# Fewer and reordered DMA transfers in a two-layer attention and SwiGLU kernel

## The chip, the core and the metric

The kernel runs on one core of a Trainium2 chip. The metric is the device time of one execution in microseconds (us); three runs of the kernel before were timed, and one execution was profiled. The core has five engines with an instruction queue each: PE (TensorE, with its weight loads shown as PEld), DVE (VectorE), ACT (ScalarE), POOL (GpSimd) and SP (SyncE, which here only issues DMA transfers). Transfers issued from SP, ACT and POOL are carried by the core's 16 DMA engines.

## The reference

Two layers of the same pair of blocks are applied to x, 2048 tokens of 1024 numbers, all in float32: softmax attention with 32 heads of 32, then a routed SwiGLU block that changes only the eight tokens with the highest router score.

```python
def _A_ref(x, wqkv, wo):
    B, S, D = x.shape
    H = 32; Dh = D // H
    qkv = (lambda x, *d: x.transpose(*d))((x @ wqkv).reshape(B, S, 3, H, Dh), 2, 0, 3, 1, 4)
    q, k, v = qkv[0], qkv[1], qkv[2]
    scale = Dh ** -0.5
    scores = jnp.einsum("bhqd,bhkd->bhqk", q, k) * scale
    p = _softmax(scores, axis=-1)
    o = jnp.einsum("bhqk,bhkd->bhqd", p, v)
    return (lambda x, *d: x.transpose(*d))(o, 0, 2, 1, 3).reshape(B, S, D) @ wo

def _B_ref(x, w_r, w_gate, w_up, w_down):
    C = 8
    r = x @ w_r
    idx = jnp.argsort(-r, axis=-1)[:, :C]
    ...
    g = _silu(x_sel @ w_gate)
    u = x_sel @ w_up
    y = (g * u) @ w_down
    r_sel = _sigmoid(jnp.take_along_axis(r, idx, axis=1))
    ...
    return x + upd.reshape(B, S, D)

x = A_x
x = x + _A_ref(_layernorm(x, axis=-1), A_wqkv, A_wo)
x = x + _B_ref(_layernorm(x, axis=-1), B_w_r, B_w_gate, B_w_up, B_w_down)
x = x + _A_ref(_layernorm(x, axis=-1), A_wqkv, A_wo)
x = x + _B_ref(_layernorm(x, axis=-1), B_w_r, B_w_gate, B_w_up, B_w_down)
```

## The kernel before

The order of the work is written out by hand: what a Python loop emits first stands first in its engine's queue. Each layer goes through three stages.

**Projections** (`steps`, 96 of them, step k, or chunk c and place b = k % 24). For each of four chunks of 512 tokens the weight matrix wqkv passes in 12 blocks of 1 MB, two steps to a block. `load_w` (L105 is its DMA, tile `wraw`) fetches a block two blocks ahead, at the even steps; ACT rounds it to a high part (L827 or L831) and POOL takes the low part (L832), and PE multiplies both with the normalised tokens (L932). Queries, keys and their low parts go back to DRAM (qh, ql, kh, kl) and come in again as `q` and `ks` for attention. Beside the projections of layer 1 the SwiGLU block of layer 0 runs (`prev`): its weights come as 1 MB tiles `fw` in five buffers (L237), in groups of four. `tick` and `refill` load a new tile for each one used; after a group of four uses at k % 4 == 3, three loads are issued there and the fourth by the `refill` of the next step.

**Attention.** 32 units, each four heads by 512 queries, against 16 blocks of 128 keys: scores (L775), exponentials on ACT (L1256), values (L1154), and row maxima ahead of time (L736). The softmax sums of a unit are formed by `sum_mm` (L1201) as one row per head, on partitions 0, 32, 64 and 96 of tile `sm`, and `store_sum` writes them to DRAM tensor `sd`. Near the end the sums are loaded in a dense form, turned into reciprocals and stored as `rd`, for each tile of 128 tokens [4, 8, 128]: four heads by eight groups by 128 tokens.

**Output projection.** 16 tiles of 128 tokens (t). `load_o(t)` brings the attention output `oT` (512 KB) and the reciprocal sums into tile `ord` (two buffers); a row of rd, 4 KB, is repeated over the 32 partitions of its head. Loads 0 to 3 are issued from SP; in the loop ACT issues the load of t + 4 right after it has rounded tile t + 2. DVE scales (L1360), ACT rounds (L1369), DVE takes the low part (L1372), PE multiplies with wo (L1438, 48 matmuls a tile into one of two PSUM buffers `pre`), and DVE adds x (L1443), takes layer-norm sums (L177), normalises (L1470) and forms the router score (L1472), whose last use frees the PSUM buffer. SP loads x for t + 2 and stores the new x for t (L1480), and between t = 1 and 4 (layer 0) or 1 and 10 (layer 1) a SwiGLU tile of 1 MB.

Of the kernel before, what the change touches and what calls it, by code (L numbers as in the profile page):

```python
# [21 lines left out]
NG = H // 4  # L22
# [31 lines left out]

KEYS_AT = [{at: slice(i * 512, i * 512 + 512) for i, at in enumerate(ats)} for ats in (
    ((1, 18), (1, 21), (2, 18), (3, 3)), ((2, 14), (2, 17), (2, 20), (3, 3)))]


def unit_events(left):
# [17 lines left out]
def tile_kernel(ctx, tc, x, wqkv, wo, w_r, w_gate, w_up, w_down, out):  # L77
# [3 lines left out]
    def sbuf(name, bufs=1, side=None):  # L81
        kw = {"side": side} if side else {}
        return tc.tile_pool(name=name, bufs=bufs, reuse_waits="tile", **kw)
# [19 lines left out]
    def dma(out, in_):  # L103
        f = [a.bitcast(F32) if a.dtype == F32R else a for a in (out, in_)]
        sync.dma_start(f[0], f[1])  # L105
# [4 lines left out]
    def ps_pre():  # L110
        return psum.tile([128, 1024], F32, name="pre", bufs=2)
# [556 lines left out]
    def layer(n, src, dst, prev=None, following=None):  # L668
# [6 lines left out]
        sd = dram.tile([NT, 4, NG, 128], F32, name=f"sd{n}")  # L675
        sd2 = dram.tile([NT, 4, NG, 128], F32, name=f"se{n}")
        rd = dram.tile([NT, 4, NG, 128], F32, name=f"rd{n}")
# [8 lines left out]
        def open_qk():  # L686
            side = "right" if prev else None
            qp = mid.enter_context(sbuf(f"q{n}", side=side))
            for i in range(3):
                QP.append(qp.tile([128, 2, 2, 512], F32R, name=f"q{i}", bufs=1))  # L690
            KS[0] = right.enter_context(sbuf(f"ks{n}", side="right")).tile([128, 2, 2, S], F32R, name="ks0")
# [9 lines left out]
        q_loads = [(b, i) for i in range(3) for b in range(2)]  # L701

        def load_q(u, j):
            g, qc = divmod(u, QC)
            if j == 0:
                Q[u] = QP[u % 3]
            b, i = q_loads[j]
            r = 64 * b + 32 * (i % 2)
            dma(Q[u][r:r + 32, :, i // 2, :],
                (ql if i == 2 else qh)[g, :, qc * 512:(qc + 1) * 512].rearrange("(p b r) c -> b r p c", p=2, b=2)[b])  # L710
# [91 lines left out]
        with ExitStack() as pst:  # L802
# [5 lines left out]
            def load_w(wb):  # L808

                RAW.append((wb, pr_.tile([128, 2048], F32, name="wraw")))  # L810
                if wb < 8:
                    w = wqkv[:, wb * 256:(wb + 1) * 256]
                else:
                    v, h = divmod(wb - 8, 2)
                    w = wqkv[h * 512:(h + 1) * 512, 2 * D + v * 512:2 * D + (v + 1) * 512]
                w = w.rearrange("(a p) c -> p a c", p=128)
                dma(RAW[-1][1].rearrange("p (a c) -> p a c", a=w.shape[1]), w)

            def split_w(parts=1):
                wb, raw = RAW.pop(0)  # L820

                wh, wl = (prev.wf.tile([128, 2048], F32R, name=i) for i in ("ord", "ohl")) if n else (
                    pr_.tile([128, 2048], F32R, name=i) for i in ("wh", "wl"))
                W[wb] = [w.rearrange("p (a c) -> p a c", a=KD if wb < 8 else 4) for w in (wh, wl)]
                sls = [slice(2048 // parts * i, 2048 // parts * (i + 1)) for i in range(parts)]
                for sl in [slice(0, 2048)] if n else []:
                    act.copy(wh[:, sl], raw[:, sl])  # L827
                    yield
                for sl in sls:
                    if not n:  # L830
                        act.copy(wh[:, sl], raw[:, sl])  # L831
                    pool.tensor_tensor(wl[:, sl], raw[:, sl], wh[:, sl].bitcast(F32), op=OP.subtract)  # L832
                    yield

            def ln_load(t):
                XT[t] = pr_.tile([128, D], F32, name="xt", bufs=4)
                for part, rows in rows_of(src, t):
                    dma(XT[t][part], rows)
# [3 lines left out]
            def ln_stat(t):  # L842
                LS[t] = ln_stats(XT[t])
# [12 lines left out]
            def ln_store(t):  # L856
                act.dma_start(xd[t], XN[t])

            def ln_quarters(t):

                for q in range(4):
                    act.dma_start(XT[t][32 * q:32 * q + 32].rearrange("r (g c) -> r g c", g=4),
                                  xd[t].rearrange("(g r) (q c) -> q r g c", g=4, q=4)[q])
# [188 lines left out]
            for k, (c, wb, i) in enumerate(steps):  # L1052
                b = k % 24
                if prev:
                    if k == 1:
                        yield
                        pw = pst.enter_context(sbuf(f"pj{n}", bufs=2))
                        routing = prev.second_stage()
                    if k >= 3:
                        next(routing, None)  # L1060
                    if k == 22:
                        moves = prev.permutation()
                    if k in (22, 23):
                        next(moves)
                    if k % 4 == 0:
                        prev.refill()
                    if k == 60:
                        assert not prev.steps
                        ln_load(NT - 1)
                        prev.close()  # L1070
                        open_qk()
                j = k // 2 + 1
                if i == 0 and j < len(blocks):
                    if j > 1:
                        list(split_w())
                        if j + 1 < len(blocks):
                            load_w(blocks[j + 1][1])

                at = b - (1, 8 if n else 7)[c == 0]
                t = 4 * (c + 1) + at // 4  # L1080
                norm = c < 3 and 0 <= at < 16
                if norm and at % 4 == 0:
                    ln_stat(t)
                    (ln_norm if n else ln_norm_split)(t)
                if norm and at % 4 == 1 and not n:
                    ln_store(t)
                if norm and at % 4 == 2 and not n:
                    ln_quarters(t)
                if wb < 8:
                    proj(wb, i, c, c == 3 and b >= 6)  # L1090
                else:
                    proj_v(wb, i, c, c == 3, norm_rest if k == 0 else None)
                if prev and k % 4 == 3 and 11 <= k < 60:
                    if prev.steps and prev.steps[0][0] == "t":
                        prev.tick()
                    for j in range(4):
                        if not (j and prev.steps and prev.steps[0][0] == "y"):
                            prev.tick()
                if norm and n and at % 4 == 2:
                    ln_tr(t, True)()  # L1100
                    if t + 4 < NT - 1:
                        ln_load(t + 4)
                if norm and not n and at % 4 == 3:
                    ln_turn(t)
                    if t + 2 < NT:
                        ln_load(t + 2)
                if (c, b) in KEYS_AT[n]:
                    for j in range(3):
                        for h in range(4):
                            load_k(0, h, j, KEYS_AT[n][c, b])  # L1110
                if (c, b) == (2, 20):
                    load_ones(0)
                    for u in range(2):
                        for j in range(len(q_loads)):
                            load_q(u, j)
            assert not pairs
        if prev:
            prev.wf_end.close()
# [3 lines left out]
        with sbuf(f"at{n}", bufs=2) as aw:  # L1122
# [87 lines left out]
            def store_sum(u, p, t):  # L1210
                (dve.tensor_copy if PLAIN <= u <= NU - 3 else act.copy)(t, p)
                g, qc = divmod(u, QC)
                for h in range(4):
                    dma(sd[4 * qc:4 * qc + 4, h, g, :], t[32 * h:32 * h + 1, :].rearrange("p (t c) -> p t c", t=4))

            def sum_out(u):
                store_sum(u, sum_mm(u), aw.tile([128, 512], F32, name="sm", bufs=1))
# [76 lines left out]
            for s in [*range(threes), *range(threes, NS, 3), *range(NS, NS + 14)]:  # L1294
# [27 lines left out]
                t = s - 1 if s < NS - LEAD else s - 2  # L1322
# [18 lines left out]
        if True:  # L1341
            OR, RD, OT, X = {}, {}, {}, {}

            def load_o(t, eng=act):
                tile = wf.tile([128, 2048], F32, name="ord").rearrange("p (k a c) -> p k a c", k=2, a=NG)
                OR[t], RD[t] = tile[:, 0], tile[:, 1]
                eng.dma_start(OR[t], oT[t])
                for h in range(4):
                    eng.dma_start(RD[t][32 * h:32 * h + 32], rd[t, h:h + 1].to_broadcast([32, NG, 128]))

            def halves_o():
                tile = wf.tile([128, 2048], F32R, name="ohl").rearrange("p (k a c) -> p k a c", k=2, a=NG)
# [70 lines left out]
            for t in range(NT - 2 if n else NT):  # L1423
                oh, ol = OT.pop(t)
                p = ps_pre()
# [61 lines left out]
        if n:  # L1487
# [3 lines left out]
            p = [[waste[:, h] for h in halves], [ps_st(), ps_pv()]]  # L1491
# [72 lines left out]
            for i in range(2):  # L1564
                t = NT - 2 + i
# [40 lines left out]
```

## Time and profile before

| | us |
|---|---|
| three runs | 4342.66, 4354.69, 4354.86 |
| median | 4354.69 |
| the profiled execution | 4348.58 |
| its span in the profile | 4346.8 |
| PE busy in the span | 4307.6 |
| POOL, DVE, ACT busy | 3270.6, 3045.8, 2880.2 |

The profile shows one execution. A row of a group gives line, engine, operation, out<-in and count, then times; "x<-y" with a q after the engine (SPq, ACTq) is a DMA that this engine's queue issued, and its length is that of the issue alone. In the rows of stretches come the stretch, its length, the busy time of PE, PEld, DVE, ACT and POOL with the number of instructions in brackets, the granted TensorE clock as a share of full speed, the mean busy share of the 16 DMA engines, and the GB/s that they moved. The chain of waits follows the work that ended last back from the last instruction; its rows give start, length and what it was.

### The profile page before, as it was taken

How to read it: one execution, taken by the hardware profiler on the slowest of the kernel's cores; microseconds unless marked ns; L12 is line 12 of the kernel's file. 1: busy time of each engine (PE TensorE's matmuls, PEld its weight loads, DVE VectorE, ACT ScalarE, POOL GpSimd, SP SyncE). 2: the span in 40 equal slices, each digit the busy share in tenths (PEclk: the TensorE clock that was granted, in tenths of full speed). 3: DMA queues.
4: the chain of work that ended last, by engine and by line, in shares of the span. 5: the costliest groups of instructions: out<-in, count | busy, mean ns of one | idle time of the engine just before them, and what ended most of it. 6: DMA issues, size and time to landing. Idle time of an engine off the chain costs nothing.

```text
span 4346.8 us, 75763 instructions
## 1 busy us (share of the span) xinstructions
PE 4307.6 (99%) x28255; PEld 2612.5 (60%) x28255; DVE 3045.8 (70%) x5607; ACT 2880.2 (66%) x3447; POOL 3270.6 (75%) x1367
## 2 busy tenths in 40 slices
PE   9999999999999999999999999999999999999998
PEld 7888755555555555558877787555555555555583
DVE  3322678888888898887422215888888888888863
ACT  3333289999999999960222222999999998999510
POOL 5544479999999999925634443899999999999152
PEclk9999999999999999999999999999999999999999
DMA  7877588998999989868698774999989999998698
GB/s 222 268 241 230 158 183 190 200 204 193 210 199 192 214 191 199 174 181 244 180 313 305 263 215 129 206 196 196 210 190 201 200 195 201 198 195 175 185 266 342
DMA packets 362638, 918.70 MB, mean 211 GB/s; under 512 B 48220, under 2 KB 184924, under 8 KB 305934
## 3 DMA queue, kind: packets, MB, share of 16 engines
q0 software_dynamic: 53312, 384.39, 44.2%
q1 hardware_dynamic: 291646, 490.07, 37.2%
q10 hardware_dynamic: 17312, 39.40, 3.3%
q8 instruction: 222, 3.64, 0.3%
q14 instruction: 146, 1.20, 0.1%
HBM read 395.35 MB, written 134.67 MB: 122 GB/s over the span
## 4 chain that ended last, share of the span: by engine, by line
PE 93%; DMA 3%; DVE 1%; issue 1%; POOL 1%; ACT 0%; SPq 0%; POOLq 0%; ACTq 0%; DVEq 0%
PE pv L1154 23%; PE pre L775 22%; PE st L932 17%; PE st L736 15%; PE pre L1438 6%; PE pre L932 5%; PE st L1201 1%; PE pv L567 1%; DMA wraw<-in_A_wqkv_dram 1%; PE pre L757 1%; PE pv L932 1%; DMA ord<-rd 0%; PE third L775 0%; DMA P<-P 0%; PE st L607 0%
## 5 line engine op out<-in xcount | busy, mean ns | idle before, releaser
L1164 POOL TENSOR_TENSOR acc<-acc,P 128x2048 f32<-128x2048 f32 x420 | 2058.7, 4902 | 9.4
L1256 ACT ACTIVATE P<-pre 128x1024 f32<-128x1024 f32 x2016 | 1955.1, 1024 | 24.8 <-PE pre L775 17.6
L743 DVE TENSOR_REDUCE nm<-st 128x1 f32<-128x512 f32 x1920 | 1321.0, 688 | 51.3 <-PE st L736 7.9
L775 PE MATMUL pre<-q,ks 64*128 64x512 f32 (+1 forms) x8064 | 1123.1, 395 | 2.4 <-ACT P L1256 2.4
L1154 PE MATMUL pv<-P,v 128*32 128x512 f32 x8192 | 1087.2, 605 | 0.0
L736 PE MATMUL st<-ks,q 64*128 64x512 f32 x2880 | 874.3, 432 | 2.0 <-issue 2.0
L775 PEld LDWEIGHTS pre<-q,ks 64*128 64x128 f32 (+1 forms) x8064 | 770.5, 186 | 159.9 <-ACT P L1256 32.1
L741 DVE CUSTOM_DVE_ANT_0 first<-st,first 128x512 f32<-128x512 f32 x960 | 664.0, 692 | 241.3 <-PE st L736 231.9
L739 ACT ACTIVATE first<-st 128x512 f32<-128x512 f32 x960 | 574.5, 598 | 184.4 <-PE st L736 99.6
L736 PEld LDWEIGHTS st<-dt,q 64*128 64x128 f32 x960 | 175.7, 183 | 798.2 <-DVE nm L741 727.4
L736 PEld LDWEIGHTS st<-ks,q 64*128 64x128 f32 x2880 | 487.9, 185 | 46.0 <-issue 2.3
L736 PE MATMUL st<-dt,q 64*128 64x512 f32 x960 | 476.3, 496 | 0.0
L1192 POOL DMA_DIRECT2D P<-P x366 | 373.9, 1022 | 111.3 <-PE st L736 39.6
L947 DVE TENSOR_TENSOR lo<-st,hi 128x512 fp32r<-128x512 f32 x128 | 88.4, 691 | 513.9 <-ACT hi L946 469.0
L832 POOL TENSOR_TENSOR ohl<-wraw,ord 128x2048 fp32r<-128x2048 f32 (+1 forms) x54 | 222.3, 4120 | 241.5 <-ACT ord L827 205.7
L946 ACT CAST hi<-st 128x512 fp32r<-128x512 f32 x128 | 75.2, 587 | 444.5 <-PE st L932 352.5
L832 POOL TENSOR_TENSOR wl<-wraw,wh 128x2048 fp32r<-128x2048 f32 (+1 forms) x54 | 222.5, 4123 | 170.6 <-ACT wh L831 165.2
L1154 PEld LDWEIGHTS pv<-P,v 128*32 128x32 f32 x8192 | 164.0, 108 | 263.7 <-issue 257.0
L1164 POOL TENSOR_TENSOR acc<-P 128x2048 f32<-128x2048 f32 x62 | 317.9, 5128 | 0.1
L181 POOL TENSOR_TENSOR rs<-mv,eps_c 128x1 f32<-128x1 f32 x64 | 27.7, 433 | 296.3 <-DVE mv L179 296.3
L1438 PE MATMUL pre<-woh,ohl 128*128 128x512 f32 x960 | 223.9, 390 | 3.0 <-DVE pre L1472 2.2
L1369 ACT CAST ohl<-ord 128x1024 fp32r<-128x1024 f32 x32 | 33.6, 1051 | 273.4 <-DVE ord L1360 114.3
(422 smaller groups left out, 5317.4 us busy)
## 6 DMA issues: line engine op xcount, KB each, us to landing
P<-P POOLq DMA_DIRECT2D x366, 1024.0 KB, 10.1
wraw<-in_A_wqkv_dram SPq DMA_DIRECT2D x96, 1024.0 KB
q<-qh SPq DMA_DIRECT2D x256, 128.0 KB
ks<-kh SPq DMA_DIRECT2D x112, 256.0 KB
fw<-in_B_w_down_dram SPq DMA_DIRECT2D x17, 1024.0 KB
vd<-vn SPq DMA_DIRECT2D x32, 512.0 KB
qh<-hi SPq DMA_DIRECT2D x64, 256.0 KB
ql<-lo SPq DMA_DIRECT2D x64, 256.0 KB
```

What stands on the lines that cost most here:

```text
L736: pe.matmul(p, Q[u][rows, i, 0, qt * 128:(qt + 1) * 128], keys, start=True, stop=True, tile_position=(64 * b, 0))
L739: act.activation(side, ps[jj], AF.Relu)
L741: dve.tensor_tensor_reduce(side, ps[jj], side, 1.0, -3.0e38, OP.add, OP.max, NM[u][:, 0, h, qt:qt + 1])
L743: dve.tensor_reduce(NM[u][:, 1 + k, h, qt:qt + 1], ps[1 - jj], axis=AX.X, op=OP.max)
L775: pe.matmul(p[:, b * 512:(b + 1) * 512], KS[(u // QC) % 2][rows, i, slot, kt * 128:(kt + 1) * 128], Q[u][rows, i, slot, :], start=(slot == ...
L832: pool.tensor_tensor(wl[:, sl], raw[:, sl], wh[:, sl].bitcast(F32), op=OP.subtract)
L932: pe.matmul(p, *pair(a, l, r), start=(a == 0 and k == 0), stop=(a == KD - 1 and k == 2))
L1154: pe.matmul(PV[u][32 * h:32 * h + 32, :], V[g, kt // 4][:, kt % 4, 32 * h:32 * h + 32], P[s][:, h, :], start=(kt == 0), stop=(kt == NT - 1 ...
L1164: (dve if on_dve else pool).tensor_tensor(o, a, P[u * NT + k].rearrange("p h c -> p (h c)"), op=OP.add)
L1192: pool.dma_start(P[u * NT + a], P[u * NT + b], accum_op=OP.add)
L1256: act.activation(P[s][:, 2 * i:2 * i + 2, :].rearrange("p h c -> p (h c)"), p, AF.Exp, scale=SCALE)
L1438: pe.matmul(p[:, bl], l[:, a, :], r[a][:, bl], start=(k == 0 and a == 0), stop=(k == 2 and a == KD - 1))
```

## The change

There are four edits. In `store_sum` the four stores of a unit, one per head, become one transfer whose source steps over the four partitions. In `load_o` the four loads of rd, one per head with 32 partitions each, become one transfer into 128 partitions. In the projections `prev.refill()` moves from ahead of `load_w` to behind it. And the loads of the first two units' queries, which stood together at step (2, 20) behind the row of ones, are spread over (2, 21), (3, 1) and (3, 7), with the ones at (3, 5).

```diff
+QUERIES_AT = {(2, 21): range(0, 4), (3, 1): range(4, 10), (3, 7): range(10, 12)}
...
-                    if k % 4 == 0:
-                        prev.refill()
                     if k == 60:
                         assert not prev.steps
                         ln_load(NT - 1)
...
                         list(split_w())
                         if j + 1 < len(blocks):
                             load_w(blocks[j + 1][1])
+                    if prev and k % 4 == 0:
+                        prev.refill()
...
-                if (c, b) == (2, 20):
+                for j in QUERIES_AT.get((c, b), ()):
+                    load_q(*divmod(j, len(q_loads)))
+                if (c, b) == (3, 5):
                     load_ones(0)
-                    for u in range(2):
-                        for j in range(len(q_loads)):
-                            load_q(u, j)
...
             def store_sum(u, p, t):
                 (dve.tensor_copy if PLAIN <= u <= NU - 3 else act.copy)(t, p)
                 g, qc = divmod(u, QC)
-                for h in range(4):
-                    dma(sd[4 * qc:4 * qc + 4, h, g, :], t[32 * h:32 * h + 1, :].rearrange("p (t c) -> p t c", t=4))
+                dma(sd[4 * qc:4 * qc + 4, :, g, :].rearrange("t h c -> h t c"),
+                    t.rearrange("(h r) (t c) -> h r t c", h=4, t=4)[:, 0])
...
                 eng.dma_start(OR[t], oT[t])
-                for h in range(4):
-                    eng.dma_start(RD[t][32 * h:32 * h + 32], rd[t, h:h + 1].to_broadcast([32, NG, 128]))
+                eng.dma_start(RD[t].rearrange("p a c -> p (a c)"),
+                              rd[t].rearrange("h a c -> h (a c)")[:, None, :].to_broadcast([4, 32, NG * 128]))
```

Lines of the file move by two or three with it. In the rows below the number behind a DRAM name is its buffer's, and the sizes are those of the destination.

ACT's queue in the output projection of layer 1, from the round of tile 3 on. Before:

```order
L1369 CAST ohl<-ord 128x1024 x2
L1347 DMA ord<-oT_21184 128x1024
L1349 DMA ord<-rd_21189 32x1024 x4
L1369 CAST ohl<-ord 128x1024
L1347 DMA ord<-oT_21184 128x1024
L1349 DMA ord<-rd_21189 32x1024 x4
```

And now:

```order
L1371 CAST ohl<-ord 128x1024 x2
L1349 DMA ord<-oT_21091 128x1024
L1350 DMA ord<-rd_21096 128x1x1024
L1371 CAST ohl<-ord 128x1024
L1349 DMA ord<-oT_21091 128x1024
L1350 DMA ord<-rd_21096 128x1x1024
```

Between two rounds ACT issues two transfers where it issued five.

SP's queue in the projections of layer 1, at one group of SwiGLU tiles. Before:

```order
L105 DMA kd_21183<-diff 128x256
L237 DMA fw<-in_B_w_up_dram 128x2048 x4
L105 DMA wraw<-in_A_wqkv_dram 128x8x256
L105 DMA qh_21178<-hi 128x512
L105 DMA ql_21179<-lo 128x512
```

And now:

```order
L108 DMA kd_21090<-diff 128x256
L240 DMA fw<-in_B_w_up_dram 128x2048 x3
L108 DMA wraw<-in_A_wqkv_dram 128x8x256
L240 DMA fw<-in_B_w_up_dram 128x2048
L108 DMA qh_21085<-hi 128x512
```

The fourth SwiGLU tile has moved behind the weight block; the first three have not.

SP's queue at the end of chunk 2 of layer 1, where keys and the first queries are loaded. Before:

```order
L105 DMA ks_25496<-kh_21180 32x512 x4
L105 DMA ks_25496<-ones_row 1x2x2048 x2
L105 DMA q_25490<-qh_21178 32x2x512 x4
L105 DMA q_25490<-ql_21179 32x2x512 x2
L105 DMA q_25491<-qh_21178 32x2x512 x4
L105 DMA q_25491<-ql_21179 32x2x512 x2
L105 DMA wraw<-in_A_wqkv_dram 128x8x256
L105 DMA vd_21182<-vn 128x4x256 x2
L105 DMA wraw<-in_A_wqkv_dram 128x8x256
```

And now:

```order
L108 DMA ks_25352<-kh_21087 32x512 x4
L108 DMA q_25346<-qh_21085 32x2x512 x4
L108 DMA wraw<-in_A_wqkv_dram 128x8x256
L108 DMA vd_21089<-vn 128x4x256 x2
L108 DMA wraw<-in_A_wqkv_dram 128x8x256
```

Four query loads are left ahead of the weight block; eight, and the two of ones, have moved to later steps.

## The prediction

> **What bounds the kernel now.** I read the page first, for the engine that sets the end.
>
> ```profile
> span 4346.8 us, 75763 instructions
> PE 4307.6 (99%) x28255; PEld 2612.5 (60%) x28255; DVE 3045.8 (70%) x5607; ACT 2880.2 (66%) x3447; POOL 3270.6 (75%) x1367
> ```
>
> TensorE is busy for 99% of the span: 39.2 us are left in which any edit can gain, and most of those are the start and the tail. So I looked for the places where this change could take from those 39 us, and then for places where it could make new ones. Busy time in stretches (stretch, length, busy of PE, PEld, DVE, ACT, POOL, granted clock, DMA share, GB/s) and the waits of PE alone (total, times, longest):
>
> ```profile
> 1000.00:1020.00 20.00, 20.00 (x158) 10.29 (x154) 17.84 (x37) 18.13 (x23) 19.92 (x8) 1.00 0.86 183
> 2255.00:2260.00 5.00, 3.30 (x24) 1.28 (x17) 3.19 (x6) 2.09 (x3) 4.78 (x2) 0.96 0.87 297
> 2260.00:2265.00 5.00, 5.00 (x18) 3.96 (x17) 0.00 (x0) 1.90 (x1) 2.81 (x2) 0.70 0.82 238
> 2570.00:2575.00 5.00, 3.66 (x16) 2.73 (x15) 0.69 (x1) 2.39 (x2) 4.01 (x2) 1.00 0.68 202
> ...
> PE st L932 <- POOL ohl L832: 2.7, 2, 1.4
> PE pre L1438 <- DVE pre L1472: 2.2, 2, 1.5
> ```
>
> In attention PE has no gap (20.00 of 20.00). In layer 1's projections it lost 1.70 us near 2257, and the clock then fell to 0.70 for 5 us (1.5 us more), and 1.34 us near 2571. The releaser both times is POOL's split of a weight block (L832). The chain of waits says what the split waited for, and the DMA issues on SP (start, length) say what stood ahead of that load:
>
> ```profile
> 2235.09 2.24 SPq L237 DMA_DIRECT2D fw<-in_B_w_up_dram  x4
> 2237.38 15.15 DMA wraw<-in_A_wqkv_dram
> 2254.54 4.57 POOL ohl L832
> ...
> 2550.19 1.21 SPq L105 DMA_DIRECT2D ks<-ones_row  x2
> 2551.44 1.81 SPq L105 DMA_DIRECT2D q<-qh  x4
> 2556.11 1.28 SPq L105 DMA_DIRECT2D q<-ql  x2
> 2557.64 8.27 DMA wraw<-in_A_wqkv_dram
> 2567.97 4.60 POOL ohl L832
> ```
>
> A weight block landed 15.15 us after 2237.38 because four SwiGLU loads of 1 MB went out just ahead of it, and another was issued only at 2557.64, behind ones and queries that began at 2550.19.
>
> The other place is the output projection, where the reciprocal sums are loaded:
>
> ```profile
> 4103.75 43.95 PE pre L1438 x192
> 4101.97 8.20 ACTq L1349 DMA_DIRECT2D ord<-rd  x4
> 4110.27 1.05 ACT L1369 CAST ohl<-ord 128x1024 fp32r<-128x1024 f32 x1 [9.98 <-DMA ord<-rd]
> 4111.35 1.23 DVE L1372 TENSOR_TENSOR ohl<-ord,ohl 128x1024 fp32r<-128x1024 f32 x1 [3.05 <-ACT ohl L1369]
> ```
>
> A tile is 48 matmuls, so PE sets a pace of 43.95 / 4 = 11.0 us a tile. ACT stood 8.20 us over four rd loads before its next copy, and DVE then waited 3.05 us for that copy. The two waits of PE for L1472 (2.2 us in all) are the end of this road: DVE works in order, L1472 is late, and the PSUM buffer that it reads and writes comes free late.
>
> How full are the DMA engines there?
>
> ```profile
> 4140.00:4220.00 80.00, 78.51 (x347) 64.69 (x347) 50.08 (x65) 8.18 (x8) 40.69 (x54) 1.00 1.02 282
> 1940.00:2060.00 120.00, 119.36 (x533) 97.22 (x532) 84.42 (x127) 11.57 (x11) 66.77 (x79) 1.00 0.89 246
> 1916.50:1918.00 1.50, 1.50 (x20) 0.51 (x16) 1.50 (x2) 0.83 (x2) 0.00 (x0) 1.00 1.12 205
> 4320.00:4330.00 10.00, 7.69 (x34) 1.59 (x32) 0.00 (x0) 0.00 (x0) 0.00 (x0) 1.00 1.03 410
> ord<-rd ACTq DMA_DIRECT2D x96, 128.0 KB
> ord<-oT ACTq DMA_DIRECT2D x24, 512.0 KB
> x<-x SPq DMA_DIRECT2D x31, 512.0 KB
> out_dram<-x SPq DMA_DIRECT2D x13, 512.0 KB
> fw<-in_B_w_gate_dram SPq DMA_DIRECT2D x16, 1024.0 KB
> ```
>
> In layer 1's output projection all 16 are full (share 1.02) at 282 GB/s, 17.6 KB/us each; in layer 0's they are at 0.89. With weights alone a full engine moves 410 / 16 = 25.6 KB/us; while little but rd loads run (1916.5 to 1918) it moves 205 / 16 = 12.8.
>
> **The change part by part.** *Weight block ahead of the fourth SwiGLU load.* The first three still go out before it; the fourth moves behind it. So the block starts one 1 MB transfer earlier, 1 MB / 297 GB/s = 3.5 us, which is more than the 1.70 us that PE lost. Gain 1.70 + 1.5 = 3.2 us (if the split stays late: 0). The moved load becomes 3.5 us later; five buffers stand for groups of four, so it is used a group later, four steps after it is issued. Without that cover it would cost up to 3.5 us in each of the ten groups.
>
> *Queries and ones spread.* The block of 2557.64 loses two ones and eight of twelve queries ahead of it: of the 7.45 us from 2550.19 to 2557.64 about 5 us, more than the 1.34 us lost. Gain 1.34 us (ends: 0 and 1.34). The four queries that the first maxima need go out at (2, 21), nine steps before (3, 6), where they are read; the rest, and the ones, have as much or more. They now stand ahead of weight blocks at (3, 2), (3, 6) and (3, 8), at most six of them; I count nothing there, since all twelve with the ones and twelve key loads cost 1.34 us where they stood together.
>
> *Stored sums as one transfer.*
>
> ```profile
> L105 SPq DMA_DIRECT2D sd<-sm x248: 552/1038/1362, 621.0 to 4058.8; - x124
> L105 SPq DMA_DIRECT2D q<-nmx x128: 537/585/1248, 516.2 to 4028.5; - x128
> L105 SPq DMA_DIRECT2D nmx<-nmr x256: 302/484/1472, 511.5 to 4026.4; - x128
> L1349 ACTq DMA_DIRECT2D ord<-rd x96: 308/432/1370, 1941.4 to 4227.2; - x96
> ```
>
> SP saves about 3 x 1.04 us a unit. Nothing waits for it: PE has 20.00 of 20.00 in attention. 0 us.
>
> *Reciprocal sums as one transfer.* Here the count of pieces matters. A transfer's issue takes at least 302 to 308 ns where its outermost count is 16 or 32 (nmx<-nmr, ord<-rd), and at least 537 to 552 where it is 2 or 4 (q<-nmx, sd<-sm). The queue handles a transfer with a small outermost count in another way. The old rd load had 32 rows outermost on both sides; the new one has 128 on the SBUF side and, in DRAM, four heads outermost, each repeated 32 times. I take the +240 ns as the mark of a transfer that only as many engines share as its outermost count allows, here four. Then 512 KB rest on four engines, 128 KB on each, where each of 16 had 32 KB.
>
> The Trainium skill, "DMA: Bandwidth & Descriptors", section "Rules for kernel authors", says the same: an outermost size below 16 confines the whole transfer to at most that many engines. The issue times above fit this rule; which engines carried what no row here shows. By the rule alone the merge would be a loss wherever the engines are nearly full.
>
> What one of the four then has to do per tile: 128 KB of rd at 25.6 or 12.8 KB/us is 5.1 to 10.2 us. Beside it, a sixteenth of oT, x in, x out and a SwiGLU load (2.5 MB, so 160 KB) at 25.6 or 17.6 KB/us is 6.4 to 9.3 us; without the SwiGLU load 96 KB, 3.8 to 5.6. Sum with SwiGLU load 11.5 to 19.5, without 8.9 to 15.8, against PE's 11.0. I take the middles, 15.5 and 12.4, since twelve engines get less to do, which speeds up what is shared, while the four read and write the rd rows in the form that ran at 205 GB/s. Excess 4.5 us (ends 0.5 and 8.5) and 1.4 us (0 and 4.8) a tile. Layer 1 has ten tiles with SwiGLU loads (t = 1 to 10) and five more rd loads: 10 x 4.5 + 5 x 1.4 = 52. Layer 0 has four (t = 1 to 4) and eleven: 18 + 15 = 33. The two ord buffers let a load go out two tiles ahead of need; of that I count one tile, 11 us, in each layer as slack that is used up first: 41 and 22, in all 63 us. Ends: 0 and (109 - 11) + (87 - 11) = 174 us. A gain belongs to it too: ACT no longer stands over four issues, so the 2.2 us of L1472 go, but a later rd puts DVE in the same wait. What is late next is the scaling on DVE (L1360), then L1472, then PE.
>
> **Sum.** The profiled execution took 4348.58 us (span 4346.8), 6.1 under the median of the three runs, 4354.69. 4348.6 - 3.2 - 1.3 + 63 = 4407 us.
>
> **Rivals.** *All 16 engines carry the merged load.* For it: both sides hold the same 128 rows, and 128 divides by 16. Against it: the issue times. Then only gains are left: 3.2 + 1.3 + 2.2 = 6.7, 4342 us, not slower. It decides if the issue of the new load stays near 0.31 us. The Trainium skill, same page and section, advises to join many small transfers into one, small meaning under 64 KB; the old loads were 128 KB, and no row here shows a gain of joining as such.
>
> *Four engines, but hidden.* If rd and the rest run at 25.6 KB/us, 10 x 0.5 + 4 x 0.5 = 7 us lie within the 22 us of slack, and 4348.6 - 4.5 = 4344 us follows. Against it: the stage ran at 17.6 KB/us with all 16 at work.
>
> *Slower still.* If rd keeps 12.8 KB/us in layer 1, 98 + 22 - 4.5 = +115 us, 4464.
>
> **How the numbers follow.** Four engines with a loss that PE sees: 0.70, of it 0.10 above 4464; hidden: 0.12; all 16: 0.18. About 0.3% (13 us) is what a measurement of this kernel can tell from no change. The hidden case and most of the all-16 case (4342, -0.15%) fall within it: 0.25; 0.05 is left for faster, 0.70 for slower. The likeliest case alone spans 4365 to 4465; with the rivals the range is 4340 to 4465.
>
> **What would show it.** Right: ord<-rd issues of 0.54 us or more; DVE ord L1360 waiting for DMA ord<-rd in tile after tile; PE busy well under 78.5 of 80 us in layer 1's output projection, with a DMA share below 1, since twelve engines idle; no wait of PE for POOL L832 near 2257 and 2571. Wrong: issues near 0.31 us and a share near 1 with PE full; a new wait for wraw or fw in the projections; a gap in attention.

## The result and the profile after

The changed kernel took 4405.51 us, the median of four runs (4403.65 to 4409.8); the old one took 4354.34, the median of four as well, the three shown above and one more. The ratio is 1.0133, with a 95% interval of 1.0116 to 1.0151: slower by 1.3%. The profiled execution took 4407.05 us. Its page:

```profile
span 4405.2 us, 75347 instructions
...
PE 4322.8 (98%) x28255; PEld 2619.4 (59%) x28255; DVE 3042.6 (69%) x5607; ACT 2882.2 (65%) x3447; POOL 3268.6 (74%) x1367
...
L1440 PE MATMUL pre<-woh,ohl 128*128 128x512 f32 x960 | 237.2, 406 | 39.7 <-DVE pre L1474 39.0
```

The work of DVE, ACT and POOL is what it was. PE is idle for 82.4 us instead of 39.2, and 39.7 us of that stand before one group, the matmuls of the output projection, where PE waits for the PSUM buffer that L1474 (L1472 before) frees. PE's busy time grew too: in the three stretches with gaps below the granted clock is 0.87, 0.96 and 0.94, in the two without 1.00. Stretches of the changed kernel (columns as above; the whole program has moved by 8 us in layer 0 and 26 us in layer 1's projections):

```profile
2275.00:2295.00 20.00, 20.00 (x105) 14.29 (x104) 6.53 (x12) 5.35 (x7) 8.39 (x6) 1.00 0.98 350
2590.00:2605.00 15.00, 15.00 (x68) 12.43 (x67) 1.38 (x2) 3.56 (x4) 5.57 (x3) 1.00 0.66 181
4180.00:4260.00 80.00, 65.70 (x253) 52.50 (x252) 40.12 (x52) 6.29 (x6) 32.68 (x41) 0.87 0.78 227
...
1940.00:2060.00 120.00, 109.08 (x465) 88.75 (x464) 71.85 (x94) 10.51 (x10) 55.08 (x69) 0.96 0.74 205
...
1740.00:1800.00 60.00, 55.67 (x412) 28.45 (x408) 47.81 (x97) 49.18 (x60) 53.74 (x20) 0.94 0.81 172
```

The first two are the places of the old stalls near 2257 and 2571, now full. In the next two, the output projections, PE lacks 14.3 of 80 and 10.9 of 120 us, and the DMA share fell from 1.02 and 0.89 to 0.78 and 0.74, although each tile needs the same bytes: PE waits for data while part of the DMA engines have nothing to do. The last is attention in layer 0, where PE lacks 4.3 us that it did not lack before.

Who waits for whom in layer 1's output projection, from the issue of the new load (minimum, median and maximum in ns, first and last start) through the waits of DVE between 4070 and 4300 to a piece of the chain of waits:

```profile
L1350 ACTq DMA_DIRECT2D ord<-rd x12: 531/531/532, 4125.1 to 4272.2; - x12
```

```profile
DVE ord L1362 <- DMA ord<-rd: 47.2, 10, 7.2
DVE ord L1362 <- DMA out_dram<-x: 16.1, 2, 8.6
```

```profile
4186.90 20.32 DMA ord<-rd
4207.28 13.08 DMA out_dram<-x
...
4245.46 22.55 DMA ord<-rd
4268.03 1.23 DVE ord L1362
...
4272.18 21.36 DMA ord<-rd
```

In these three places a rd load is on its way for 20 to 23 us, where PE needs a tile every 11. DVE's scaling (L1362) waits for it ten times, 47.2 us in all. Stores of x stand in the same chain, the one shown with 13 us. They would be late for the same reason if a part of each must pass the busy engines too; which engines carried a store no row shows.

Where the 58.4 us of span went is read from the first and last start of the matmuls of the loop in each layer, before and then after:

```profile
L1438 PE MATMUL pre<-woh,ohl x512: 387/389/500, 1920.5 to 2095.4; 128*128 128x512 f32 x171
L1438 PE MATMUL pre<-woh,ohl x448: 387/389/502, 4079.9 to 4232.5; 128*128 128x512 f32 x150
```

```profile
L1440 PE MATMUL pre<-woh,ohl x512: 387/389/765, 1928.5 to 2121.4; 128*128 128x512 f32 x171
L1440 PE MATMUL pre<-woh,ohl x448: 387/389/767, 4095.7 to 4281.9; 128*128 128x512 f32 x150
```

| stretch | before | after | difference |
|---|---|---|---|
| start to layer 0's output projection | 1920.5 | 1928.5 | +8.0 |
| layer 0's output projection | 174.9 | 192.9 | +18.0 |
| from there to layer 1's | 1984.5 | 1974.3 | -10.2 |
| layer 1's output projection | 152.6 | 186.2 | +33.6 |
| from there to the end of the span | 114.3 | 123.3 | +9.0 |

The last +9.0 belongs to the rd loads as well: the products of the last two tiles stand behind the loop, and their data come late. Of the kernels below, the one with the merged load alone (merged_only) has 121.7 us there, the changed one with four rd loads again (four_loads) 114.4.

### The profile page after: what moved, and what is told of

Read it like the earlier page. It is cut to its first block, busy times and chain, and to the rows that moved or that the text cites. A ratio compares the mean times of both kernels' runs of the same rounds, so it can differ in the third digit from the quotient of the medians.

```text
span 4405.2 us, 75347 instructions
## 1 busy us (share of the span) xinstructions
PE 4322.8 (98%) x28255; PEld 2619.4 (59%) x28255; DVE 3042.6 (69%) x5607; ACT 2882.2 (65%) x3447; POOL 3268.6 (74%) x1367
## 4 chain that ended last, share of the span: by engine, by line
PE 86%; DMA 8%; DVE 2%; issue 2%; POOL 1%; ACT 0%; SPq 0%; POOLq 0%; ACTq 0%; DVEq 0%
PE pv L1156 22%; PE pre L778 21%; PE st L935 17%; PE st L739 14%; PE pre L935 6%; DMA ord<-rd 3%; DMA out_dram<-x 2%; PE st L1203 1%; DMA x<-x 1%; PE pre L1440 1%; DMA P<-P 1%; PE pv L570 1%; PE pre L760 1%; DMA x<-in_A_x_dram 1%; PE pv L935 1%
## 5 line engine op out<-in xcount | busy, mean ns | idle before, releaser
L746 DVE TENSOR_REDUCE nm<-st 128x1 f32<-128x512 f32 x1920 | 1320.8, 688 | 53.8 <-PE st L739 10.9
L184 POOL TENSOR_TENSOR rs<-mv,eps_c 128x1 f32<-128x1 f32 x64 | 37.1, 580 | 360.9 <-DVE mv L182 360.9
L1440 PE MATMUL pre<-woh,ohl 128*128 128x512 f32 x960 | 237.2, 406 | 39.7 <-DVE pre L1474 39.0
L1371 ACT CAST ohl<-ord 128x1024 fp32r<-128x1024 f32 x32 | 33.6, 1051 | 334.6 <-DVE ord L1362 308.1
```

Source lines behind the costliest of these rows:

```text
L746: dve.tensor_reduce(NM[u][:, 1 + k, h, qt:qt + 1], ps[1 - jj], axis=AX.X, op=OP.max)
L1440: pe.matmul(p[:, bl], l[:, a, :], r[a][:, bl], start=(k == 0 and a == 0), stop=(k == 2 and a == KD - 1))
```

## The experiments

The theory: a transfer's outermost count sets how many DMA engines share it, always the same ones, and with a count of 4 the four of them are busy for longer than PE's 11 us a tile. Rivals: one large transfer that signals only as a whole comes too late, whoever carries it; or the other edits have a part in the loss.

**The changed kernel with four rd loads** (four_loads).

```diff
-                eng.dma_start(RD[t].rearrange("p a c -> p (a c)"),
-                              rd[t].rearrange("h a c -> h (a c)")[:, None, :].to_broadcast([4, 32, NG * 128]))
+                for h in range(4):
+                    eng.dma_start(RD[t][32 * h:32 * h + 32], rd[t, h:h + 1].to_broadcast([32, NG, 128]))
```

> The changed kernel with the four rd loads per tile of the old kernel, its other three edits kept. If the whole loss is the merged rd load (engines theory): 4.5 us of gain are left, 4350 us beside 4354.5, a ratio of 0.999, PE back to over 78 of 80 us in layer 1's output projection, no wait of PE near 2257 and 2571. If part of the loss belongs to the moved refill, the queries or the joined stores of the sums: slower than the old kernel by that part; the 4.3 us in which PE waited for q near 1770 in the changed kernel would then be there again.

4347.72 us beside 4351.56, ratio 0.9995 (0.9985 to 1.0006). The loss is gone, so it is the rd load's. The 4.5 us of gain can't be told from nothing, and PE's wait for q near 1770 stayed (4.3 us): that part does not belong to the rd load.

**The old kernel with the merged rd load alone** (merged_only): the reverse of that diff, applied to the old kernel.

> The old kernel with the one merged rd load per tile, nothing else changed. If the engines that carry the merged load are the whole cause: the loss of the changed kernel and its missing gains of 4.5 us, so +51 to +56 us, 4406 to 4410, and the waits near 2257 and 2571 are there as before. If the edits only lose together: less than +30 us.

4409.86 us, ratio 1.0141 (1.0122 to 1.0161), +58 us: the one edit brings the whole loss, somewhat more than expected. One thing came otherwise: of the two old stalls at weight blocks only the second is there (1.8 us, near 2597). The first is gone, though this kernel has neither the moved refill nor the spread queries.

**One transfer, 16 rows outermost** (copies_16). The 512 KB into 128 partitions stay one transfer; only the source is laid out differently.

```diff
-        rd = dram.tile([NT, 4, NG, 128], F32, name=f"rd{n}")
+        rd = dram.tile([NT, 4, 4, NG, 128], F32, name=f"rd{n}")
...
-                dma(half_of(rd, i), t)
+                for k in range(4):
+                    dma(rd[i * 8:i * 8 + 8, :, k].rearrange("t h (a g) c -> (t h) a (g c)", a=4), t)
...
-                              rd[t].rearrange("h a c -> h (a c)")[:, None, :].to_broadcast([4, 32, NG * 128]))
+                              rd[t].rearrange("h k a c -> (h k) (a c)")[:, None, :].to_broadcast([16, 8, NG * 128]))
```

> The changed kernel, but rd is stored four times in DRAM, so that the one load per tile reads 16 rows, each repeated 8 times: still one transfer of 512 KB into 128 partitions, outermost count 16 in place of 4. If the outermost count limits how many engines carry a transfer: 16 carry it, the issue takes near 0.31 us, no loss is left, 4345 to 4352 us. If one large transfer as such lands too late (it signals only when all of it is there), whatever carries it: like the changed kernel, about 4405. The three more stores of 128 KB, twice a layer, cost at most 2 us at the start of each output projection.

4345.67 us, ratio 0.9992 (0.9980 to 1.0003). No loss is left, with one transfer as large as the one that cost 58 us. The rival of the large transfer falls. The issue time, though, did not behave as expected (below).

**Eight rows outermost** (copies_8): the same with two copies, `[8, 16, NG * 128]`.

> As with four copies, but rd is stored twice, and the load reads 8 rows, each repeated 16 times: outermost count 8. By the outermost count, 8 engines have 64 KB of rd a tile: 2.5 to 5 us beside 6.4 to 9.3 us of other work with a SwiGLU load, middle 11.6 against PE's 11.0, and below it without; 14 tiles x 0.6 = 8 us lie within the slack, so about 4350, and a landing between those of 4 and 16. If the number of engines is all or nothing (16 or 4): about 4405, with a landing as in the changed kernel. If one large transfer as such is the cause: 4405 too, but then also with outermost count 16.

4359.79 us, ratio 1.0018 (1.0005 to 1.0030): 10 us more than expected, but nearly all of the loss is gone, as eight engines with a little too much to do would have it.

**Four transfers, each with four rows outermost** (four_by_four). From the 16-row kernel:

```diff
-                eng.dma_start(RD[t].rearrange("p a c -> p (a c)"),
-                              rd[t].rearrange("h k a c -> (h k) (a c)")[:, None, :].to_broadcast([16, 8, NG * 128]))
+                for h in range(4):
+                    eng.dma_start(RD[t][32 * h:32 * h + 32].rearrange("p a c -> p (a c)"),
+                                  rd[t, h].rearrange("k a c -> k (a c)")[:, None, :].to_broadcast([4, 8, NG * 128]))
```

> rd stored four times as in the kernel with 16 rows outermost, the changed kernel otherwise; the rd load of a tile is four transfers again, one per head with 32 partitions and 128 KB, but each reads 4 rows repeated 8 times, outermost count 4. If an outermost count of 4 puts every such transfer on the same four engines: 128 KB on each of the four as with the merged load, so a loss like the changed kernel's, 4395 to 4415 us, although there are four transfers. If successive transfers go to different engines: 32 KB on each of 16, 4345 to 4352. If the loss came from joining four transfers into one: 4345 to 4352 as well.

4406.35 us, ratio 1.0135 (1.0115 to 1.0154), the loss of the changed kernel, with as many transfers, of the same size and into the same partitions, as in the old one. Joining is not what costs; the outermost count is, and four transfers in a row used the same engines.

**Two transfers, each with two rows outermost** (two_by_two), in the old kernel:

```diff
-                for h in range(4):
-                    eng.dma_start(RD[t][32 * h:32 * h + 32], rd[t, h:h + 1].to_broadcast([32, NG, 128]))
+                for i in range(2):
+                    eng.dma_start(RD[t][64 * i:64 * i + 64].rearrange("p a c -> p (a c)"),
+                                  rd[t, 2 * i:2 * i + 2].rearrange("h a c -> h (a c)")[:, None, :].to_broadcast([2, 32, NG * 128]))
```

> The old kernel with two rd transfers per tile, each for two heads and 64 partitions, outermost count 2 in the source. If both go to the same two engines: 256 KB on each of two, 10.2 to 20.5 us beside 6.4 to 9.3 us (3.8 to 5.6 without a SwiGLU load), middles 23 and 20 us a tile against 11.0: 14 x 12 + 16 x 9 - 22 = 290 us, about 4640. If the two transfers go to different pairs: 128 KB on each of four, about 4405 as with one merged transfer. If fewer engines don't matter: 4354.

4571.42 us, ratio 1.0521 (1.0504 to 1.0537), +222 us: as if the same two engines carried both, though by less than the 290 us worked out.

The pace of the tiles gives the price. L1443 (L1445 to L1447 in the others) runs once a tile; its rows for layer 0 and layer 1, from the first to the last start, of the old kernel, the changed one, and those with 16, 8, four by 4 and two by 2 rows:

```profile
L1443 DVE TENSOR_TENSOR x<-pre,x x16: 1205/1224/1226, 1932.6 to 2103.1; 128x1024 f32<-128x1024 f32 x16
L1443 DVE TENSOR_TENSOR x<-pre,x x14: 1218/1224/1225, 4092.4 to 4236.5; 128x1024 f32<-128x1024 f32 x14
```

```profile
L1445 DVE TENSOR_TENSOR x<-pre,x x16: 1205/1224/1225, 1940.7 to 2129.2; 128x1024 f32<-128x1024 f32 x16
L1445 DVE TENSOR_TENSOR x<-pre,x x14: 1217/1224/1226, 4108.4 to 4294.8; 128x1024 f32<-128x1024 f32 x14
```

```profile
L1446 DVE TENSOR_TENSOR x<-pre,x x16: 1204/1225/1226, 1940.7 to 2111.1; 128x1024 f32<-128x1024 f32 x16
L1446 DVE TENSOR_TENSOR x<-pre,x x14: 1217/1225/1225, 4090.3 to 4231.7; 128x1024 f32<-128x1024 f32 x14
```

```profile
L1446 DVE TENSOR_TENSOR x<-pre,x x16: 1205/1225/1226, 1935.3 to 2107.5; 128x1024 f32<-128x1024 f32 x16
L1446 DVE TENSOR_TENSOR x<-pre,x x14: 1218/1225/1226, 4093.6 to 4246.3; 128x1024 f32<-128x1024 f32 x14
```

```profile
L1447 DVE TENSOR_TENSOR x<-pre,x x16: 1201/1220/1225, 1941.2 to 2139.1; 128x1024 f32<-128x1024 f32 x16
L1447 DVE TENSOR_TENSOR x<-pre,x x14: 1217/1220/1225, 4122.3 to 4300.5; 128x1024 f32<-128x1024 f32 x14
```

```profile
L1444 DVE TENSOR_TENSOR x<-pre,x x16: 1202/1220/1225, 1937.7 to 2203.5; 128x1024 f32<-128x1024 f32 x16
L1444 DVE TENSOR_TENSOR x<-pre,x x14: 1218/1221/1225, 4189.8 to 4445.8; 128x1024 f32<-128x1024 f32 x14
```

| kernel | outermost count | rd KB a tile on each engine, by the theory | us a tile, layer 0 (of 15) | us a tile, layer 1 (of 13) |
|---|---|---|---|---|
| old, four transfers | 32 | 32 | 11.4 | 11.1 |
| copies_16, one | 16 | 32 | 11.4 | 10.9 |
| copies_8, one | 8 | 64 | 11.5 | 11.7 |
| changed, one | 4 | 128 | 12.6 | 14.3 |
| four_by_four, four | 4 | 128 | 13.2 | 13.7 |
| two_by_two, two | 2 | 256 | 17.7 | 19.7 |

From the changed kernel to two_by_two each of the engines has 128 KB more, and a tile takes 5.1 us (layer 0) and 5.4 us (layer 1) longer: 24 to 26 KB/us (128 KB are 131,072 bytes). The profiled execution of two_by_two was 14 us under its median, so the step may be half a us a tile larger. What is left of a tile is 12.6 - 5.1 = 7.5 and 14.3 - 5.4 = 8.9 us of other work. With 64 KB that gives 10.1 and 11.6; the first was 11.5, since even the old kernel needs 11.4 there, and the second was 11.7. At these points the time follows the bytes on the busiest engine.

The profiles also show how many engines were at work. Stretches of layer 1's output projection in which the rd load was waited for, of the changed kernel (two), copies_8, four_by_four and two_by_two:

```profile
4118.00:4124.00 6.00, 0.98 (x5) 0.48 (x3) 1.79 (x2) 1.04 (x1) 0.00 (x0) 0.96 0.26 96
4204.00:4206.00 2.00, 2.00 (x11) 1.65 (x10) 0.43 (x1) 0.00 (x0) 0.10 (x1) 1.00 0.24 94
4121.00:4123.00 2.00, 2.00 (x11) 1.65 (x10) 2.00 (x3) 0.30 (x1) 0.00 (x0) 1.00 0.48 123
4141.00:4143.00 2.00, 2.00 (x6) 1.54 (x6) 2.00 (x3) 0.00 (x0) 0.00 (x0) 0.50 0.25 99
4216.00:4226.00 10.00, 10.00 (x40) 8.12 (x39) 2.45 (x4) 1.05 (x1) 0.00 (x0) 0.87 0.13 51
```

The DMA share stands near 4/16 = 0.25 with a count of 4, whether in one transfer or in four, near 8/16 with 8, and at 2/16 = 0.13 for 10 us with two transfers of count 2. So only as many engines worked as the outermost count says, and successive transfers shared them. In two_by_two each of the two moved 51 / 2 = 25.5 KB/us.

**The other edits.** Only the joined stores of the sums, in the old kernel (stores_only), and only the moved refill and the spread queries (refill_queries):

```diff
-                for h in range(4):
-                    dma(sd[4 * qc:4 * qc + 4, h, g, :], t[32 * h:32 * h + 1, :].rearrange("p (t c) -> p t c", t=4))
+                dma(sd[4 * qc:4 * qc + 4, :, g, :].rearrange("t h c -> h t c"),
+                    t.rearrange("(h r) (t c) -> h r t c", h=4, t=4)[:, 0])
```

> The old kernel with only the four stores of a unit's sums joined to one. As predicted: no change, 4354 us, a ratio of 1.000. If the joined stores bring the gap that PE has at the query loads near 1770 in each kernel that has them: it is there again, PE 4 us under full, and the time is 3 to 5 us over the old kernel's; the gains near 2257 and 2571 are not there.

> The old kernel with the moved refill and the spread queries alone (four stores of sums, four rd loads). As predicted: 4.5 us faster, about 4350, a ratio of 0.999, PE full near 2257 and 2571. If the gap at the query loads near 1770 belongs to the joined stores: it is gone here. If it belongs to these two edits: it is there.

4352.8 us, ratio 1.0009 (0.9998 to 1.0019), for the stores; 4345.57 us, ratio 0.9994 (0.9983 to 1.0005), for the other two, both beside 4349.56. Neither can be told from no change by its time. The traces tell more: PE's waits and the stretch 1740 to 1800 of stores_only, then that stretch of refill_queries and its places of the two old stalls.

```profile
PE st L736 <- DMA q<-qh: 8.8, 4, 2.3
...
PE st L932 <- POOL ohl L832: 3.6, 2, 2.0
```

```profile
1740.00:1800.00 60.00, 55.78 (x408) 28.12 (x404) 47.60 (x96) 49.12 (x60) 53.48 (x19) 0.94 0.81 172
```

```profile
1740.00:1800.00 60.00, 60.00 (x463) 30.73 (x463) 54.74 (x111) 55.52 (x68) 59.36 (x22) 1.00 0.82 173
2250.00:2270.00 20.00, 20.00 (x105) 14.25 (x105) 6.29 (x11) 5.06 (x6) 9.55 (x6) 1.00 0.90 305
2565.00:2580.00 15.00, 15.00 (x68) 12.41 (x67) 1.39 (x2) 3.26 (x4) 5.87 (x3) 1.00 0.73 176
```

With the joined stores PE lacks 4.2 us there, the clock falls to 0.94, and layer 0's output projection starts 7.4 us later than before (1927.9); the stalls behind the split of a weight block (L832) are still there. With the other two edits PE is full in all three places. A wait for q (3.4 us) did come elsewhere, in layer 1's attention, so such gaps can come without joined stores too; the place near 1770 shows one only with them.

**Towards a better kernel.** The 16-row load with the moved refill and the spread queries, but four stores of the sums (copies_16_apart), and the 16-row load alone in the old kernel (copies_16_alone); the edits are those shown above.

> The kernel with rd stored four times and loaded with 16 rows outermost, with the moved refill and the spread queries, but with four stores of the sums per unit as in the old kernel. If the joined stores cost what the profiles of the kernels with them show (layer 0's output projection starts 7 to 8 us later, 1927.9 to 1928.6 beside 1920.5): 3 to 7 us faster than the same kernel with joined stores, about 4341, a ratio of 0.997 to 0.998, and the start of layer 0's output projection near 1921. If such gaps come anywhere by chance: 4345 to 4348, ratio 0.999, and a gap at some other query load.

> The old kernel with only the rd load changed: rd stored four times, one load per tile with 16 rows outermost. If one transfer in place of four has a gain of its own (ACT no longer stands 8 us over four issues, layer 1's output projection took 149.9 us with it beside 152.6): 2 to 4 us faster, ratio 0.999. If the three more stores take that back: 1.000, within 2 us.

copies_16_apart took 4340.52 us beside 4351.07, ratio 0.9985 (0.9974 to 0.9996): faster than the old kernel by a little, the only one here whose interval lies below 1. Layer 0's output projection starts at 1921.1, and PE has no wait for q left. Beside the same kernel with joined stores (copies_16, 0.9992) the gain is within the intervals, so it shows in the trace but not for certain in the time. copies_16_alone took 4348.5 us, ratio 0.9995 (0.9985 to 1.0005): one transfer in place of four of 128 KB, with three more stores of rd, has no gain that could be measured.

## Why the prediction was right, step by step

**Reciprocal sums (+63 predicted).** The mechanism held: four engines carry the load, the scaling on DVE comes late, then L1474, then PE. The size: 18.0 us in layer 0 (22 predicted), 33.6 + 9.0 = 42.6 in layer 1 (41), in all 60.6; merged_only has 25.3, 28.6 and 7.4, in all 61.3. The mean of the tiles was predicted as (10 x 15.5 + 5 x 12.4) / 15 = 14.5 us in layer 1 and (4 x 15.5 + 11 x 12.4) / 15 = 13.2 in layer 0, and was 14.3 and 12.6.

Two things in that step were wrong, and a third is not shown. First, its evidence: the issue time is no mark of the number of engines. The rd loads of copies_16, copies_8, four_by_four and two_by_two were issued in

```profile
L1351 ACTq DMA_DIRECT2D ord<-rd x12: 522/522/1172, 4099.0 to 4215.2; - x12
```

```profile
L1351 ACTq DMA_DIRECT2D ord<-rd x12: 598/598/599, 4105.6 to 4232.7; - x12
```

```profile
L1352 ACTq DMA_DIRECT2D ord<-rd x48: 613/614/1129, 4137.0 to 4289.7; - x48
```

```profile
L1349 ACTq DMA_DIRECT2D ord<-rd x10: 489/506/3736, 4211.9 to 4281.9; - x10
```

so 522 ns with a count of 16 and no loss, and 506 with a count of 2 and the largest loss. The four have in common that a row is repeated in the middle of the pattern, and all take longer than the 308 ns of the old load. The sign named, 0.54 us or more, was met by 0.531 only nearly, and it would not have told the cases apart. The conclusion was right, and what bore it was the rule that stood beside it: the Trainium skill, "DMA: Bandwidth & Descriptors", section "Rules for kernel authors". The runs agree with it at 2, 4, 8 and 16 (+222, +51 to +58, +8 and -6 us). The Trainium skill says on the same page, section "Why a DMA increments its semaphore by 16 and not by 1", which engines these are: a transfer issued from SP or ACT takes the lowest-numbered of the 16 (seen there for counts of 16, 10, 2 and 1). four_by_four and two_by_two agree in that successive transfers share their engines (DMA shares of 0.25 and 0.13); no run shows the numbers of the engines.

Second, the rate of the rd rows. I took the middle between 25.6 and 12.8 KB/us, 7.7 us for 128 KB; two_by_two puts it at 5.1 to 5.4. That is a reason why 290 us were expected there and 222 came. In the forecast this was made good by the other work: taken at 7.9 us with a SwiGLU tile and 4.7 without, on average 5.5 in layer 0 and 6.8 in layer 1, where 7.5 and 8.9 were found. One error of about +2.4 us a tile and one of about -2.0 cancelled: that the mean of a tile came out so close is luck.

Third, the difference that a SwiGLU tile makes (4.5 us of excess with, 1.4 without), and the slack of 11 us a layer. In layer 0 only the tiles 1 to 4 have a SwiGLU load. Starts of L1443 and L1445 in tiles 0 to 4 and 4 to 15, before and after:

```profile
L1443 DVE TENSOR_TENSOR x<-pre,x x5: 1221/1225/1226, 1932.6 to 1976.2; 128x1024 f32<-128x1024 f32 x5
L1443 DVE TENSOR_TENSOR x<-pre,x x12: 1205/1224/1225, 1976.2 to 2103.1; 128x1024 f32<-128x1024 f32 x12
```

```profile
L1445 DVE TENSOR_TENSOR x<-pre,x x5: 1218/1224/1224, 1940.7 to 1990.2; 128x1024 f32<-128x1024 f32 x5
L1445 DVE TENSOR_TENSOR x<-pre,x x12: 1205/1224/1225, 1990.2 to 2129.2; 128x1024 f32<-128x1024 f32 x12
```

They lost 49.5 - 43.6 = 5.9 us, the others 139.0 - 126.9 = 12.1. By the forecast it would be 4 x 4.5 - 11 = 7 and 11 x 1.4 = 15, so the sums are near. But that is 1.5 and 1.1 us a tile, and the loss did not wait for the slack to be used up: the first step alone, from tile 0 to tile 1, went from 10.7 to 14.6 us, and in layer 1 from 11.0 to 18.2. Neither term is shown tile by tile.

**Weight block and queries (-4.5).** Both stalls are gone from the changed kernel and from refill_queries, as forecast. For the weight block that does not show the edit at work: the first stall is gone from merged_only and two_by_two too, which do not have the edit. For the queries it fits better: the second stall stands in all five kernels without the edits and in none of the seven with them; but four_loads has a stall of 2.0 us at a later weight block (near 2612), whose load was issued behind twelve key loads. copies_16_alone, without the edits, waits 6.7 us for weight blocks. The 10.2 us between the output projections are not these edits' either. That stretch, 1984.5 us in the old kernel, is 1976.9 in merged_only and 1977.4 in two_by_two, without the edits, and 1983.4 in four_loads and 1981.5 in refill_queries, with them. One part is known: the old kernel's profile has a stall in layer 1's attention, `PE st L736 <- issue: 2.0, 1, 2.0`, that the changed one does not have. The rest is open. As a time, the gain of the two edits is not shown (0.9983 to 1.0005).

**Stored sums (0).** This step failed in the trace. The edit was put at nothing because PE had no gap in one stretch of attention; it made one: PE waited 4.3 us for the queries near 1770, the granted clock of 0.94 over the 60 us of that stretch is worth some 3.6 more (60 x 0.06, an estimate), and layer 0's output projection began 8.0 us later. The gap stands at this place in all six kernels with joined stores, smaller only in copies_8 (1.3 us of waiting), and in none of the six without them, where the stretch is full. What happens there is open. The DMA rows for 1750 to 1767, before and after, show the load of instructions that falls into these query loads (queue, packets, MB, share of 16 engines):

```profile
q8 instruction: 1, 0.02, 0.4%
```

```profile
q8 instruction: 1, 0.02, 0.9%
```

0.9% of 16 x 17 us is 2.4 us for one packet, where it took 1.1. So the two met, but whether the one delayed the other was not tried. By time the joined stores cost -0.02% to +0.19%.

**L1472's wait (2.2 us, counted as not gained).** Right: it became 39.0 us.

**The sum.** 60.6 + 8.0 - 10.2 = 58.4 us of span, where 58.5 were predicted. The main term fell 2.4 us short. The rest agrees by luck: +8.0 was not foreseen, 5.7 more than forecast was gained in a stretch that varies by as much without the edits, and the two nearly cancel.

**The rivals.** All 16 engines: copies_16 is that case and gives nearly what was said of it (4342, measured 4345.67), but the kernel as written is not that case. Four engines but hidden: not with four, and almost with eight. Slower still (4464): it needed 12.8 KB/us for the rd rows, and they ran at 24 to 26. Of the signs named, the waits of DVE, the idle PE, the fallen DMA share and the full PE at the two old stalls came as said; the gap in attention, named as a sign against, came too, and belongs to the joined stores.

## What to carry to other kernels

When transfers are joined, look at the outermost dimension of both sides before the size: a broadcast written as heads x repeats has the heads outermost, and here it put all of its bytes on as many engines as there are heads, the same ones each time. Cost such a transfer by the busiest engine (its own bytes, and a sixteenth of all else) against the pace of the consumer, and if it must be one transfer, lay the source out so that 16 rows stand outermost. In a stage with nearly full DMA engines, a low mean DMA share together with late loads is the sign of it, and a share that stands near 4/16 or 2/16 while a load is awaited tells the number.

## What was not expected of the hardware

Four transfers in a row with an outermost count of 4 behaved like one: 1.0135 beside 1.0133. Halving the engines from four to two cost 5.1 to 5.4 us a tile, 24 to 26 KB/us for each engine, while rd loads with all 16 engines had run at 12.8 KB/us each in the old kernel. And the least issue time of a rd load from ACT rose from 308 ns to between 489 and 613 ns where a row is repeated in the middle of its pattern, without following the count.
